# Fewer changes of tile shape on TensorE, a reordered start and a reordered tail in a six-layer cross network

## Chip, cores, metric

One core of one Trainium2 chip. The metric is device time in microseconds (us). All runs quoted are in the fast state. Before: 514.48 us, median of 13 runs (513.51 to 515.35).

## The reference

```python
B, F, D, L = 16384, 26, 16, 6          # Din = 416
def reference(x0, ws, bs):             # x0 (16384, 416), ws (6, 416, 416), bs (6, 416), all bf16
    x = x0
    for l in range(6):
        proj = jnp.einsum('bd,de->be', x, ws[l]) + bs[l]
        x = x0 * proj + x
    return x
```

The activations are kept transposed, with the 416 features on the partitions: 416 = 3 x 128 + 32. The three planes of 128 fill the partitions. The last 32 features of four groups of 512 rows are stacked into one tile of 128 partitions, so four small matmuls can run side by side in different parts of the TensorE array (in the profile of before, eight 32*128 ones take 0.54 us: two passes of 0.216 and a change of tile shape of 0.11).

## The kernel before

The rows are worked in 4 blocks of 4096, each block in two halves q of 2048 rows; 4 blocks x 6 layers x 2 halves = 48 *sets*. A set has four *phases* m: three that make 128 output features each, and one (m = 3) that makes the last 32.

```python
if m == 0:
    ...                                     # wait for x of this set
if m < 3:
    k32_first = (m == 1)
    def full_part(first):                   # "F": 12 matmuls 128*128, 4 banks x 3 planes
        for j in range(4):
            if first: bank_wait(slots[j])
            for c in range(3):
                pe.matmul(pb[:, bk, :], w_sb[:, l, c, 128*m:128*(m+1)], src12[:, c, tcols(q, j)], ...)
    def k32_part(first):                    # "K": 4 matmuls 32*128, side by side
        if first:
            for slot in slots: bank_wait(slot)
        for j in range(4):
            pe.matmul(pb[:, bk, :], w3rep[32*j:32*(j+1), l, 128*m:128*(m+1)],
                      src3[32*j:32*(j+1), pcols(q)], ..., tile_position=(32*j, 0))
    ...                                     # K then F if k32_first, else F then K
else:
    ...                                     # "D": 4 matmuls 32*32, side by side
    ...                                     # then "C": 12 matmuls 128*32, four side by side
mm.then_inc(s_pe, 1)
```

ScalarE (ACT) evicts each phase from PSUM and adds the bias; VectorE (DVE) makes x0 * proj, then adds x, in place. The start and the tail, in the issuing programs:

```python
# scalar: weights, then all staging of the last 32 features (64-byte rows), then the bias
dma_weights(act, 0, s_w0)
dma_staging(act, 0, 0)
dma_staging(act, 0, 1)
act.wait_ge(s_peb, 1); act.activation(bias_f, pb[...], Copy)
# sync: transposed planes of x0
for c in range(3): dma_plane(sp, 0, 0, c)
sp.wait_ge(s_w0, 16 * NW0)
for c in range(3): dma_plane(sp, 0, 1, c)
...
# tail: the last set (set 47) is transposed on TensorE and evicted in 16 pieces, in two halves of 8;
# the set before it (46) is transposed by DMA: 3 planes, then 4 small pieces, then a 640 KB store
for h in range(2):
    for c in range(4):
        ...
        tr = pe.transpose(tb[:, 128*c:128*(c+1)], xT[kbL][:, c, cols], ident128)   # per tile
```

## Time and profile before

| | before |
|---|---|
| time, median | 514.48 us |
| span of the profiled run | 512.5 us |
| TensorE (PE) busy / DVE / ACT | 94% / 73% / 63% |
| first real matmul | 13.96 us |
| steady pair of sets | 2 x 9.94 us |
| tail after the dense stream | 19 us |

"PE" rows are matmuls, and their ends are modelled, so times between matmuls are read from start to start. The profile lines themselves, with how to read them, are shown in the prediction below.

### The profile page before, as it was taken

To read this page: it belongs to the slowest core of one execution; us is meant where nothing else is said; L and a number is where in the kernel's file an instruction comes from. 1 tells how busy PE (TensorE), PEld (TensorE's weight loads), DVE (VectorE), ACT (ScalarE), POOL (GpSimd) and SP (SyncE) were. 2 spreads that over 40 slices of the span, in tenths; PEclk is the share of its full clock that TensorE was granted. 3 is DMA by queue.
4 is the path that set the end of the run, shared out by engine and by line. 5 is a ranking of instruction groups with operands and counts; after the bars stand their busy time and mean duration, and the time that the engine had idled before them with its cause. 6 is when DMAs were issued, how large, how long until landed. Compare 5 with 4: busy or idle time off the path is not lost.

```text
span 512.5 us, 7691 instructions
## 1 busy us (share of the span) xinstructions
PE 480.8 (94%) x3101; PEld 193.6 (38%) x3149; DVE 376.5 (73%) x402; ACT 323.5 (63%) x254; POOL 0.9 (0%) x8
## 2 busy tenths in 40 slices
PE   1999999999999999999999999999999999999972
PEld 0333433433333343343334334333433433343332
DVE  0278779768867877887787788778778877877872
ACT  1366666666667666666766666676666667666651
POOL 0000000000000000000000000000000000000000
PEclk9999999999999999999999999999999999999985
DMA  9869200000975880000669691000459400000186
GB/s 175 189 143 165 62 3 1 0 1 4 207 136 139 177 142 1 1 1 1 123 153 203 117 175 33 0 1 3 82 137 198 119 1 0 2 1 0 20 191 190
DMA packets 149551, 42.26 MB, mean 82 GB/s; under 512 B 130054, under 2 KB 149516, under 8 KB 149516
## 3 DMA queue, kind: packets, MB, share of 16 engines
q1 hardware_dynamic: 144688, 41.07, 39.0%
q10 hardware_dynamic: 4828, 0.69, 0.9%
q8 instruction: 25, 0.41, 0.3%
q14 instruction: 10, 0.08, 0.1%
HBM read 3.61 MB, written 13.63 MB: 34 GB/s over the span
## 4 chain that ended last, share of the span: by engine, by line
PE 93%; issue 2%; DMA 1%; SPq 1%; DVE 1%; DVEq 0%
PE pb L384 74%; PE pb L402 8%; PE pb L434 7%; PE pb L423 3%; DMA x0Ta<-in_x_dram 1%; SPq L171 1%; PE pb L461 1%; DVE xTb L554 0%; DVE x0Ta L580 0%; DVE t1M L540 0%; PE pb L467 0%; DVE t L545 0%; DVEq L184 0%; DVEq L538 0%
## 5 line engine op out<-in xcount | busy, mean ns | idle before, releaser
L497 ACT ACTIVATE projMa<-pb,bias_f 128x2048 bf16<-128x2048 f32 (+1 forms) x90 | 144.4, 1625 | 84.8 <-issue 44.0
L497 ACT ACTIVATE projMb<-pb,bias_f 128x1536 bf16<-128x1536 f32 (+2 forms) x108 | 147.1, 1396 | 78.1 <-issue 45.1
L384 PE MATMUL pb<-xTa,w_sb 128*128 128x512 bf16 x700 | 158.0, 379 | 3.1 <-issue 3.0
L384 PE MATMUL pb<-xTb,w_sb 128*128 128x512 bf16 x700 | 157.8, 379 | 3.2 <-issue 3.2
L384 PEld LDWEIGHTS pb<-xTb,w_sb 128*128 128x128 bf16 x720 | 67.2, 98 | 92.5 <-issue 17.0
L384 PEld LDWEIGHTS pb<-xTa,w_sb 128*128 128x128 bf16 x720 | 67.1, 98 | 92.6 <-issue 17.0
L554 DVE TENSOR_TENSOR xTb<-t1M,xTb 128x2048 bf16<-128x2048 bf16 x60 | 73.2, 1220 | 13.9 <-PE pb L434 13.9
L554 DVE TENSOR_TENSOR xTa<-t1M,xTa 128x2048 bf16<-128x2048 bf16 x60 | 73.2, 1220 | 13.8 <-PE pb L434 13.8
L540 DVE TENSOR_TENSOR t1M<-projMa,x0Ta 128x2048 bf16<-128x2048 bf16 x36 | 43.9, 1219 | 23.0 <-ACT projMa L497 23.0
L540 DVE TENSOR_TENSOR t1M<-projMb,x0Tb 128x2048 bf16<-128x2048 bf16 x36 | 44.0, 1221 | 19.2 <-ACT projMb L497 19.2
L540 DVE TENSOR_TENSOR t1M<-projMb,x0Ta 128x2048 bf16<-128x2048 bf16 x36 | 44.0, 1221 | 18.6 <-ACT projMb L497 18.3
L540 DVE TENSOR_TENSOR t1M<-projMa,x0Tb 128x2048 bf16<-128x2048 bf16 x36 | 43.9, 1220 | 17.4 <-ACT projMa L497 17.4
L384 PE MATMUL pb<-x0Ta,w_sb 128*128 128x512 bf16 x140 | 34.0, 397 | 1.5 <-DMA x0Ta<-in_x_dram 1.1
L384 PE MATMUL pb<-x0Tb,w_sb 128*128 128x512 bf16 x140 | 31.6, 379 | 0.6 <-issue 0.6
L384 PEld LDWEIGHTS pb<-x0Ta,w_sb 128*128 128x128 bf16 x144 | 13.9, 101 | 21.5 <-issue 5.7
L384 PEld LDWEIGHTS pb<-x0Tb,w_sb 128*128 128x128 bf16 x144 | 13.4, 98 | 18.5 <-issue 3.4
L402 PE MATMUL pb<-xT3b,w3rep 32*128 32x512 bf16 x240 | 20.1, 381 | 0.0
L402 PE MATMUL pb<-xT3a,w3rep 32*128 32x512 bf16 x240 | 20.1, 381 | 0.0
L554 DVE TENSOR_TENSOR xTa<-t1M,x0Ta 128x2048 bf16<-128x2048 bf16 x12 | 14.7, 1221 | 3.0 <-PE pb L434 3.0
L434 PE MATMUL pb<-xTb,w_sb 128*32 128x512 bf16 x240 | 16.6, 383 | 0.0
L434 PE MATMUL pb<-xTa,w_sb 128*32 128x512 bf16 x240 | 16.6, 383 | 0.0
L554 DVE TENSOR_TENSOR xTb<-t1M,x0Tb 128x2048 bf16<-128x2048 bf16 x12 | 14.6, 1220 | 2.7 <-PE pb L434 2.7
(54 smaller groups left out, 161.2 us busy)
## 6 DMA issues: line engine op xcount, KB each, us to landing
out_dram<-ostage SPq DMA_DIRECT2D x7, 1024.0 KB, 6.7
out_dram<-ostage SPq DMA_DIRECT2D x7, 640.0 KB, 4.3
out_dram<-x0Ta SPq DMA_DIRECT2D x2, 832.0 KB, 6.8
w_sb<-in_ws_dram SPq DMA_DIRECT2D x5, 312.0 KB, 2.8
st<-in_x_dram SPq DMA_DIRECT2D x24, 32.0 KB, 2.5
w3rep<-in_ws_dram SPq DMA_DIRECT2D x20, 26.0 KB, 2.2
w_sb<-in_ws_dram ACTq DMA_DIRECT2D x1, 312.0 KB
st<-in_x_dram ACTq DMA_DIRECT2D x8, 32.0 KB, 5.6
```

Of the source, the lines that this page charges most:

```text
L171: eng.dma_start_transpose(out=x0T[kb][:, c, qcols(q)], in_=x0[r0:r0 + QC, 128 * c:128 * (c + 1)]).then_inc(s_x0[kb][q], 16)
L384: r = pe.matmul(pb[:, bk, :], w_sb[:, l, c, 128 * m:128 * (m + 1)], src12[:, c, tcols(q, j)], start=(first and c == 0), stop=((not first) ...
L402: r = pe.matmul(pb[:, bk, :], w3rep[32 * j:32 * (j + 1), l, 128 * m:128 * (m + 1)], src3[32 * j:32 * (j + 1), pcols(q)], start=first, stop ...
L423: mm = pe.matmul(pb[32 * j:32 * (j + 1), bk, :], w3rep[32 * j:32 * (j + 1), l, 384:416], src3[32 * j:32 * (j + 1), pcols(q)], start=True, ...
L434: mm = pe.matmul(pb[32 * j:32 * (j + 1), bk, :], w_sb[:, l, c, 384:416], src12[:, c, tcols(q, j)], start=False, stop=(c == 2), tile_positi ...
L461: tr = pe.transpose(tb[:, 128 * c:128 * (c + 1)], xT[kbL][:, c, cols], ident128[:, :])
L497: act.activation(dst, src, ACTF.Identity, bias=bias_f[:, l, m:m + 1], scale=1.0).then_inc(s_act, nb)
L540: dve.tensor_tensor(t1M[:, m, :], projM[par][:, m, :], x0T[kb][:, m, qcols(q)], ALU.mult,).then_inc(s_op1, 1)
L554: dve.tensor_tensor(xT[kb][:, m, qcols(q)], t1M[:, m, :], src12[:, m, qcols(q)], ALU.add,).then_inc(s_dve, 1)
```

## The change

Its intent: let parts with the same tile shape meet, so that TensorE changes shape less often; keep transfers that are not yet needed out of the way of the first ones; and shorten the tail by sending the last 160 columns of set 46 through TensorE too ("hybrid") and by evicting set 47 in one batch of eight double tiles.

```diff
+ORDER, START, HYB, BATCH = 1, 1, 1, 1
+STAGE0, ORDER10, OP3, WARM = 1, 1, 1, 0
+LATE, STAGE1, PLANES = 0, 0, 0
...
-                    for m in range(4):
+                    if not ORDER:
+                        order = [(0, False), (1, True), (2, False), (3, True)]
+                    elif ORDER10 and sidx > 0 and sidx % 2 == 0:
+                        order = [(0, True), (1, False), (2, True), (3, False)]
+                    elif sidx % 2 == 0:
+                        order = [(0, False), (1, True), (2, False), (3, False)]
+                    else:
+                        order = [(3, True), (0, False), (1, True), (2, False)]
+                    for m, small_first in order:
...
                 dma_weights(act, 0, s_w0)
-                dma_staging(act, 0, 0)
-                dma_staging(act, 0, 1)
+                if STAGE0 or not (START or STAGE1):
+                    dma_staging(act, 0, 0)
+                if not (START or STAGE1):
+                    dma_staging(act, 0, 1)
                 act.wait_ge(s_peb, 1)
                 ...                                  # the bias
+                if START or STAGE1:
+                    ...
+                    dma_staging(act, 0, 1)
...
-                sp.wait_ge(s_w0, 16 * NW0)
+                if START or PLANES:
+                    sp.wait_ge(s_x0[0][0], 16 * 3)
+                else:
+                    sp.wait_ge(s_w0, 16 * NW0)
...                                                   # tail, TensorE
+                if HYB:
+                    pe.wait_ge(s_dve, baseH + 4)
+                ...                                   # 16 + 16 transposes of set 46 into 4 banks
+                halves = [range(OSUB)] if BATCH else [range(0, 8), range(8, 16)]
+                ...                                   # set 47, plane by plane, two tiles to a bank
+                if BATCH:
+                    tr.then_inc(s_pt, 1)              # one signal after all 64
...                                                   # tail, ScalarE
+                for g in range(NP46):                 # 4 evictions 128x640 into the staging tile
...                                                   # VectorE: fourth product earlier in odd sets (OP3)
```

More of the change, by code (lines that the diff above doesn't have):

```diff
@@ L82, in bass_standalone__cross_network_dcn__recsys_kernel @@
         s_outB = sem("s_outB")
+        s_p46 = sem("s_p46")
+        s_ev46 = sem("s_ev46")
         s_pt = sem("s_pt")
@@ L87, in bass_standalone__cross_network_dcn__recsys_kernel @@
         phases = []
+        phase_of = {}
         nslot = 0
+        sidx = 0
         for k in range(NBLK):
@@ L95, in bass_standalone__cross_network_dcn__recsys_kernel @@
                         nslot += nb
-                        phases.append(dict(k=k, l=l, q=q, m=m, slots=slots))
+                        ph = dict(k=k, l=l, q=q, m=m, slots=slots, small_first=small_first)
+                        phases.append(ph)
+                        phase_of[(sidx, m)] = ph
+                    sidx += 1
         act_val_after_slot = {}
@@ L114, in bass_standalone__cross_network_dcn__recsys_kernel @@
             ph["act_after"] = acc
-        tslots = list(range(nslot, nslot + OSUB))
-        nslot += OSUB
-        ev_engine = ["A" if jj % 8 in (1, 4, 7) else "D" for jj in range(OSUB)]
+        NP46 = 4 if HYB else 0
+        p46slots = list(range(nslot, nslot + NP46))
+        nslot += NP46
+        NTB = OSUB // 2 if BATCH else OSUB
+        tslots = list(range(nslot, nslot + NTB))
+        nslot += NTB
+        ev_engine = ["D", "A", "D", "D", "A", "D", "D", "A"]
+        if not BATCH:
+            ev_engine = ["A" if jj % 8 in (1, 4, 7) else "D" for jj in range(OSUB)]
         ev_index = []
         na = nd = 0
-        for jj in range(OSUB):
-            if ev_engine[jj] == "A":
+        for i in range(NTB):
+            if ev_engine[i] == "A":
                 ev_index.append(na)
@@ L127, in bass_standalone__cross_network_dcn__recsys_kernel, with op_pos @@
                 nd += 1
-        N_EVA, N_EVD = na, nd
+        def op_pos(s):
+            return (0, 1, 3, 2) if OP3 and s % 2 else (0, 1, 2, 3)
         def slot_free_wait(eng, slot):
@@ L135, in slot_free_wait @@
                 eng.wait_ge(s_act, act_val_after_slot[prev])
-            else:
-                jj = prev - tslots[0]
-                if ev_engine[jj] == "A":
-                    eng.wait_ge(s_evA, ev_index[jj] + 1)
+            elif prev in p46slots:
+                eng.wait_ge(s_ev46, p46slots.index(prev) + 1)
+            else:
+                i = prev - tslots[0]
+                if ev_engine[i] == "A":
+                    eng.wait_ge(s_evA, ev_index[i] + 1)
                 else:
-                    eng.wait_ge(s_evD, ev_index[jj] + 1)
+                    eng.wait_ge(s_evD, ev_index[i] + 1)
         def qcols(q):
@@ L154, in bass_standalone__cross_network_dcn__recsys_kernel @@
         sLAST = NSETS - 1
+        sHYB = set_index(NBLK - 1, L - 1, 0) if HYB else -1
         NOUT = NBLK * NQ
@@ L221, in _ @@
                 ).then_inc(s_bias, 1)
+                if START or STAGE1:
+                    if not STAGE0:
+                        dma_staging(act, 0, 0)
+                    dma_staging(act, 0, 1)
                 act.wait_ge(s_bias, 1)
@@ L249, in _ @@
                             for h in range(2):
-                                na_h = sum(1 for jj in range(8 * h + 8) if ev_engine[jj] == "A")
-                                nd_h = sum(1 for jj in range(8 * h + 8) if ev_engine[jj] == "D")
+                                nh = (h + 1) * (NTB // 2)
+                                na_h = sum(1 for i in range(nh) if ev_engine[i] == "A")
+                                nd_h = sum(1 for i in range(nh) if ev_engine[i] == "D")
                                 sp.wait_ge(s_evA, na_h)
                                 sp.wait_ge(s_evD, nd_h)
+                                if LATE and h == 0:
+                                    sp.wait_ge(s_ev46, 4)
+                                    sp.dma_start(
+                                        out[r0 - QC:r0, 256:D].rearrange("(j a) d -> a j d", a=128),
+                                        ostage[:, :, 256:D],
+                                    ).then_inc(s_outB, 16)
                                 sp.dma_start(
@@ L261, in _ @@
                             continue
-                        last = False
+                        hyb = sL == sHYB
                         base = 4 * sL
@@ L278, in _ @@
                         ntr += 2
-                        if not last:
+                        if not hyb:
                             sp.wait_ge(s_dve, base + 3)
@@ L292, in _ @@
                         n_stA += 1
-                        if not last:
+                        if hyb and LATE:
+                            pass
+                        elif hyb:
+                            sp.wait_ge(s_ev46, 4)
+                            sp.dma_start(
+                                orows[:, 256:D].rearrange("(j a) d -> a j d", a=128),
+                                ostage[:, :, 256:D],
+                            ).then_inc(s_outB, 16)
+                        else:
                             sp.wait_ge(s_dve, base + 4)
@@ L355, in _ @@
                     s = set_index(k, l, q)
-                    if m == 0:
+                    if ip % 4 == 0:
                         if l == 0:
                             pe.wait_ge(s_x0[kb][q], 16 * 3 * (k // 2 + 1))
+                            if m != 0 or ph["small_first"]:
+                                pe.wait_ge(s_c3, NQ * k + q + 1)
                         else:
@@ L374, in _ @@
                     if m < 3:
-                        k32_first = (m == 1)
+                        k32_first = ph["small_first"]
                         def full_part(first):
@@ L394, in k32_part @@
                             r = None
-                            if l == 0 and m == 0:
+                            if l == 0 and ip % 4 == 0 and not first:
                                 pe.wait_ge(s_c3, NQ * k + q + 1)
@@ L421, in _ @@
                         bk = slots[0] % NBANK
-                        for j in range(4):
-                            mm = pe.matmul(
-                                pb[32 * j:32 * (j + 1), bk, :],
-                                w3rep[32 * j:32 * (j + 1), l, 384:416],
-                                src3[32 * j:32 * (j + 1), pcols(q)],
-                                start=True,
-                                stop=False,
-                                tile_position=(32 * j, 32 * j),
-                                skip_group_check=True,
-                            )
@@ L432, in _, with diag_part @@
-                        for c in range(3):
+                        diag_first = ph["small_first"]
+                        def diag_part(first):
+                            r = None
                             for j in range(4):
-                                mm = pe.matmul(
+                                r = pe.matmul(
                                     pb[32 * j:32 * (j + 1), bk, :],
-                                    w_sb[:, l, c, 384:416],
-                                    src12[:, c, tcols(q, j)],
-                                    start=False,
-                                    stop=(c == 2),
-                                    tile_position=(0, 32 * j),
+                                    w3rep[32 * j:32 * (j + 1), l, 384:416],
+                                    src3[32 * j:32 * (j + 1), pcols(q)],
+                                    start=first,
+                                    stop=(not first),
+                                    tile_position=(32 * j, 32 * j),
@@ L441, in _, with col_part @@
                                     skip_group_check=True,
                                 )
+                            return r
+                        def col_part(first):
+                            r = None
+                            for c in range(3):
+                                for j in range(4):
+                                    r = pe.matmul(
+                                        pb[32 * j:32 * (j + 1), bk, :],
+                                        w_sb[:, l, c, 384:416],
+                                        src12[:, c, tcols(q, j)],
+                                        start=(first and c == 0),
+                                        stop=((not first) and c == 2),
+                                        tile_position=(0, 32 * j),
+                                        skip_group_check=True,
+                                    )
+                            return r
@@ L443, in _ @@
+                        if diag_first:
+                            diag_part(True)
+                            mm = col_part(False)
+                        else:
+                            col_part(True)
+                            mm = diag_part(False)
                         mm.then_inc(s_pe, 1)
@@ L447, in _ @@
                 kbL = kL % 2
-                baseL = 4 * sLAST
-                for h in range(2):
-                    for c in range(4):
-                        if h == 0:
-                            pe.wait_ge(s_dve, baseL + c + 1)
-                        for jj in range(8 * h, 8 * h + 8):
-                            slot = tslots[jj]
-                            bk = slot % NBANK
-                            tb = pb[:, bk, :].bitcast(BF16)
-                            if c == 0:
-                                slot_free_wait(pe, slot)
-                            cols = slice(qL * QC + jj * 128, qL * QC + (jj + 1) * 128)
-                            if c < 3:
+                baseH = 4 * sHYB
@@ new lines, in _ @@
+                if HYB:
+                    pe.wait_ge(s_dve, baseH + 4)
+                for g in range(NP46):
+                    slot_free_wait(pe, p46slots[g])
+                for c in (2, 3):
+                    for g in range(NP46):
+                        bk = p46slots[g] % NBANK
+                        tb = pb[:, bk, :].bitcast(BF16)
+                        tr = None
+                        for u in range(4):
+                            jj = 4 * g + u
+                            off = u * 256
+                            if c == 2:
+                                cols = slice(jj * 128, (jj + 1) * 128)
@@ L461, in _ @@
                                 tr = pe.transpose(
-                                    tb[:, 128 * c:128 * (c + 1)], xT[kbL][:, c, cols], ident128[:, :]
+                                    tb[:, off:off + 128], xT[kbL][:, 2, cols], ident128[:, :]
                                 )
                             else:
-                                j = jj // 4
-                                pc = slice(qL * TN + (jj % 4) * 128, qL * TN + (jj % 4 + 1) * 128)
+                                pc = slice((jj % 4) * 128, (jj % 4 + 1) * 128)
@@ L467, in _ @@
                                 tr = pe.matmul(
-                                    tb[:, 384:D],
-                                    xT3[kbL][32 * j:32 * (j + 1), pc],
-                                    ident128[32 * j:32 * (j + 1), 32 * j:32 * (j + 1)],
+                                    tb[:, off + 128:off + 160],
+                                    xT3[kbL][32 * g:32 * (g + 1), pc],
+                                    ident128[32 * g:32 * (g + 1), 32 * g:32 * (g + 1)],
                                     is_transpose=True,
-                                    tile_position=(32 * j, 0),
+                                    tile_position=(32 * g, 0),
@@ L473, in _, with warm @@
                                 )
+                        if c == 3:
+                            tr.then_inc(s_p46, 1)
+                baseL = 4 * sLAST
+                tr = None
+                def warm(n):
+                    for i in range(n):
+                        pe.matmul(
+                            pb[:, tslots[0] % NBANK, 256:512],
+                            w_sb[:, 0, 0, 0:128],
+                            w_sb[:, 0, i % 3, 0:256],
+                            start=True,
+                            stop=True,
+                        )
@@ new lines, in _ @@
+                halves = [range(OSUB)] if BATCH else [range(0, 8), range(8, 16)]
+                for c, jj in [(c, jj) for hv in halves for c in range(4) for jj in hv]:
+                    if jj == 0:
+                        if WARM and c == 0:
+                            slot_free_wait(pe, tslots[0])
+                        if WARM and c < 3:
+                            warm(10 if c == 0 else 8)
+                        pe.wait_ge(s_dve, baseL + c + 1)
+                    if True:
+                        slot = tslots[jj // 2] if BATCH else tslots[jj]
+                        bk = slot % NBANK
+                        off = (jj % 2) * TN if BATCH else 0
+                        tb = pb[:, bk, :].bitcast(BF16)
+                        if c == 0 and (jj % 2 == 0 or not BATCH):
+                            slot_free_wait(pe, slot)
+                        cols = slice(qL * QC + jj * 128, qL * QC + (jj + 1) * 128)
+                        if c < 3:
+                            tr = pe.transpose(
+                                tb[:, off + 128 * c:off + 128 * (c + 1)],
+                                xT[kbL][:, c, cols],
+                                ident128[:, :],
+                            )
+                        else:
+                            j = jj // 4
+                            pc = slice(qL * TN + (jj % 4) * 128, qL * TN + (jj % 4 + 1) * 128)
+                            tr = pe.matmul(
+                                tb[:, off + 384:off + D],
+                                xT3[kbL][32 * j:32 * (j + 1), pc],
+                                ident128[32 * j:32 * (j + 1), 32 * j:32 * (j + 1)],
+                                is_transpose=True,
+                                tile_position=(32 * j, 0),
+                            )
+                            if not BATCH:
@@ L483, in _ @@
                     if s >= 2:
-                        act.wait_ge(s_op1, 4 * (s - 2) + m + 1)
+                        act.wait_ge(s_op1, 4 * (s - 2) + op_pos(s - 2)[m] + 1)
                     col0 = 0
@@ L500, in _ @@
                         col0 += nb
-                for jj in range(OSUB):
-                    if ev_engine[jj] != "A":
+                if HYB:
+                    act.wait_ge(s_outB, 16 * (NOUT - 2))
+                for g in range(NP46):
+                    bk = p46slots[g] % NBANK
+                    tb = pb[:, bk, :].bitcast(BF16)
+                    act.wait_ge(s_p46, g + 1)
+                    act.activation(
+                        ostage[:, 4 * g:4 * (g + 1), 256:D],
+                        tb[:, 0:1024].rearrange("p (u e) -> p u e", e=256)[:, :, 0:160],
+                        ACTF.Copy,
+                    ).then_inc(s_ev46, 1)
+                if BATCH:
+                    act.wait_ge(s_pt, 1)
+                for i in range(NTB):
+                    if ev_engine[i] != "A":
                         continue
-                    bk = tslots[jj] % NBANK
+                    bk = tslots[i] % NBANK
                     tb = pb[:, bk, :].bitcast(BF16)
-                    act.wait_ge(s_pt, jj + 1)
-                    act.activation(ostageL[:, jj, :], tb[:, 0:D], ACTF.Copy).then_inc(s_evA, 1)
+                    if not BATCH:
+                        act.wait_ge(s_pt, i + 1)
+                        act.activation(ostageL[:, i, :], tb[:, 0:D], ACTF.Copy).then_inc(s_evA, 1)
+                        continue
+                    act.activation(
+                        ostageL[:, 2 * i:2 * i + 2, :],
+                        tb[:, 0:1024].rearrange("p (u e) -> p u e", e=TN)[:, :, 0:D],
+                        ACTF.Copy,
+                    ).then_inc(s_evA, 1)
             @block.vector
@@ L533, in _ @@
                     src3 = x0T3[kb] if l == 0 else xT3[kb]
+                    pos = op_pos(s)
                     def op1(m):
-                        dve.wait_ge(s_act, phases[4 * s + m]["act_after"])
+                        dve.wait_ge(s_act, phase_of[(s, m)]["act_after"])
                         if s >= 1:
@@ L551, in op2 @@
                             dve.wait_ge(s_pe, 4 * s + 4)
-                        dve.wait_ge(s_op1, 4 * s + m + 1)
+                        dve.wait_ge(s_op1, 4 * s + pos[m] + 1)
                         if m < 3:
@@ L565, in _ @@
                     op2(0)
+                    if OP3 and s % 2:
+                        op1(3)
                     op1(2)
                     op2(1)
-                    op1(3)
+                    if not (OP3 and s % 2):
+                        op1(3)
                     op2(2)
@@ L573, in _ @@
                         c3_transpose(k + 1, 1)
-                for jj in range(OSUB):
-                    if ev_engine[jj] != "D":
+                if BATCH:
+                    dve.wait_ge(s_pt, 1)
+                for i in range(NTB):
+                    if ev_engine[i] != "D":
                         continue
-                    bk = tslots[jj] % NBANK
+                    bk = tslots[i] % NBANK
                     tb = pb[:, bk, :].bitcast(BF16)
-                    dve.wait_ge(s_pt, jj + 1)
-                    dve.tensor_copy(ostageL[:, jj, :], tb[:, 0:D]).then_inc(s_evD, 1)
+                    if not BATCH:
+                        dve.wait_ge(s_pt, i + 1)
+                        dve.tensor_copy(ostageL[:, i, :], tb[:, 0:D]).then_inc(s_evD, 1)
+                        continue
+                    dve.tensor_copy(
+                        ostageL[:, 2 * i:2 * i + 2, :],
+                        tb[:, 0:1024].rearrange("p (u e) -> p u e", e=TN)[:, :, 0:D],
+                    ).then_inc(s_evD, 1)
 _INS = ['x0', 'ws', 'bs']
```

## The prediction

The sum in it came to 8.1 us, so 506.4. What no trace or run of this case shows is cut, and each cut is marked. One term of the sum: the 0.6, the estimate for a rise of the clock that might come earlier at the start. Without it the terms make 7.5, so 507.0. Rival (b) is that a change of shape between some pairs costs less, or more, than between the rest.

> **What bounds the kernel now.** I began with the page's busy table and its slices.
>
> ```profile
> PE 480.8 (94%) x3101; PEld 193.6 (38%) x3149; DVE 376.5 (73%) x402; ACT 323.5 (63%) x254; POOL 0.9 (0%) x8
> PE   1999999999999999999999999999999999999972
> PE 93%; issue 2%; DMA 1%; SPq 1%; DVE 1%; DVEq 0%
> ```
>
> TensorE (PE) is full from the second slice to the last two, and the third line, the chain that ended last, is TensorE for 93%. The view of waits has no TensorE wait for ScalarE, VectorE or a PSUM bank in the steady part, so only fewer TensorE microseconds, an earlier first matmul or a shorter tail can help. DVE (73%) and ACT (63%) are followers.
>
> Next the timeline of TensorE alone, one steady set (2048 rows of one layer; there are 48):
>
> ```profile
> 203.79 0.40 PE L423 MATMUL pb<-xT3b,w3rep 32*32 32x512 bf16 x4
> 204.12 0.83 PE L434 MATMUL pb<-xTb,w_sb 128*32 128x512 bf16 x12
> 205.11 2.54 PE L384 MATMUL pb<-xTb,w_sb 128*128 128x512 bf16 x11 [0.16 <-issue]
> 207.58 0.61 PE L402 MATMUL pb<-xT3b,w3rep 32*128 32x512 bf16 x8
> 208.12 5.35 PE L384 MATMUL pb<-xTb,w_sb 128*128 128x512 bf16 x24
> 213.41 0.40 PE L402 MATMUL pb<-xT3b,w3rep 32*128 32x512 bf16 x4
> 213.73 0.40 PE L423 MATMUL pb<-xT3b,w3rep 32*32 32x512 bf16 x4
> 214.06 0.83 PE L434 MATMUL pb<-xTb,w_sb 128*32 128x512 bf16 x12
> ```
>
> Read start to start, since matmuls overlap. Call the tile shapes F (128*128), K (32*128), D (32*32) and C (128*32); four K, D or C run side by side and cost one pass. F x24 takes 213.41 - 208.12 = 5.29 us = 24 passes + one change of shape; K x8 takes 208.12 - 207.58 = 0.54 = 2 passes + one change. The difference, 22 passes, is 4.75: a pass is 0.216 us and a change 0.11. A set is 36 F + 3 K + 1 D + 3 C = 43 passes = 9.28, and has 6 changes (F-K, K-F, F-K, K-D, D-C, C-F) = 0.66; the sum, 9.94, is the period seen from 204.12 to 214.06. So a set holds 0.66 us in which nothing is multiplied. That is the only slack inside TensorE.
>
> The start, from the chain in order of time and the DMA view between 12.3 and 13.0 us (packets of a queue, MB, share of 16 engines; packets overlap, so shares pass 100%):
>
> ```profile
> 6.53 7.38 DMA x0Ta<-in_x_dram
> 13.96 4.85 PE pb L384 x12
> q10 hardware_dynamic: 1533, 0.10, 149.8%
> q1 hardware_dynamic: 40, 0.00, 3.9%
> ```
>
> The first matmul waits for the third transposed plane of x0, which lands at 13.9. The next two lines show why so late: the plane's data are moved by about 12.3, but then queue 10, which carries the 64-byte rows of staging, has the engines, and queue 1, with the completion writes of that plane, gets 3.9%. Staging of the second half (q=1), which is not needed yet, stands in front. The second line also shows a half-speed start: 12 passes in 4.85 us where 2.6 are due.
>
> The tail, from the timeline (SPq is the queue that issues transfers) and the windows (us, busy time of PE, PEld, DVE, ACT, POOL, TensorE clock, DMA share, GB/s):
>
> ```profile
> 494.70 6.95 SPq L296 DMA_TRANSPOSE ostage<-xT3b  x4
> 502.80 0.38 SPq L302 DMA_DIRECT2D out_dram<-ostage  x1
> 503.27 2.57 SPq L254 DMA_DIRECT2D out_dram<-x0Ta  x2
> 503.30 1.50 DVE L580 COPY x0Ta<-pb 128x416 bf16<-128x416 bf16 x5 [2.33 <-PE pb L467]
> 496.00:498.00 2.00, 1.03 (x8) 0.77 (x8) 2.00 (x3) 0.00 (x0) 0.00 (x0) 0.52 1.09 314
> 508.00:509.00 1.00, 0.00 (x0) 0.00 (x0) 0.00 (x0) 0.00 (x0) 0.00 (x0) 0.50 1.12 333
> ```
>
> The dense stream ends at T = 493.2 and the span at 512.5, so the tail is 19.3 us. The first half of the last set is evicted by 501.0, but its store leaves only at 503.27: the issuing queue was held by four DMA transposes of the set before and by that set's 640 KB store. From 504 to 511.8 the DMA engines then move 2.3 MB without a hole. TensorE's clock drops to half at about 496[...].
>
> [...]
>
> **The change, part by part.** (1) Order of phases. With | between phases, an even set becomes K F|F K|K F|C D (the very first F K|K F|F K|C D) and an odd one D C|F K|K F|F K. Neighbouring sets now meet D to D and K to K. Changes per pair: K-F, F-K, K-F, F-C, C-D in the even set, D-C, C-F, F-K, K-F, F-K in the odd one: 10 in place of 12. Passes stay 86. In the whole run 48 x 5 = 240 changes replace 48 x 5 + 47 = 287: 47 x 0.11 = 5.2 us, all on the path. I take F-C as costly as C-F (0.11), though the trace has not got it.
>
> Can the followers keep up? I laid one pair out by hand. It takes 86 x 0.216 + 10 x 0.11 = 19.65 us. A phase of a K first needs all four banks at once, freed by the eviction of two phases back (1.97 us, or 2.12 in two pieces). The tightest case: the even set's first phase ends at 2.9, ScalarE is done at about 5.1, and the third phase's K asks at 5.8. The margin is about 0.7 us, and the same elsewhere. On VectorE an even set's last add is done about 15.3 and an odd one's about 6 us into the next pair, each some 4 us before use; the swap of the fourth product in odd sets follows the order in which ScalarE delivers. So nothing is given back here.
>
> (2) Start. Staging of q=1 is issued after the bias, and the q=1 planes only after the q=0 planes have landed. The third plane's completion is then written at about 12.3 and not 13.0: 0.7 us gained. The q=1 planes took from 13.0 to 20.0 and will take until about 22; they are needed at 25, so this is hidden. [...]
>
> (3) Tail, counted from the new T. The last set now ends with an F K phase, whose eviction ends at T+2.1, so VectorE's planes come at T+1.6, 4.5, 5.6 and 6.0 (now T+1.25, 3.5, 5.0, 5.3): later by 0.4 to 1.0. TensorE does 32 transposes of the previous set's last columns in about 1.6 us while it would idle. ScalarE evicts them in 4 x about 0.6 (0.41 per 128x416 now, scaled to 640) by T+4.6. Their 640 KB leave at T+5 rather than T+9.6, with four or five DMA transposes fewer. The last set's 64 transposes come plane by plane: plane 0 done at T+4.8, as half of its banks wait for those ScalarE evictions; planes 1 and 2, 16 x 0.107 each at the half clock, T+6.5 and T+8.2; the small ones T+8.75. All evictions now start there, twice as large: three on VectorE at no more than 2 x 0.284 give the first half at T+10.5. The store's data begin 1.2 us after its issue (502.8 to 504.0 now), 1.7 MB at 325 GB/s take 5.2, and 0.7 passes between the data's end and the span's end: T+17.7 against T+19.3. Gain 1.6.
>
> Sum: 5.2 + 0.7 + 0.6 + 1.6 = 8.1, so 514.5 - 8.1 = 506.4.
>
> **The rivals.** (a) A wait takes the place of the switches: PSUM banks or ScalarE, with a margin of only 0.7 us, stop the K-first phases. Against it: ACT idles a third of the time, and waits for TensorE, not the reverse. If it came, 0.3 us in each pair would cost 7 and the time would be 513. (b) [...] C-F measures 0.11 to 0.12, so I expect no surprise. If F-C were free, 24 x 0.11 = 2.6 more would come: 504. (c) The tail gives back: one semaphore for all 64 transposes puts every eviction after the last of them, where halves overlapped before. If ScalarE's four evictions or the cold clock hold plane 0 longer, the tail's gain is lost: 508. If the clock stays high, planes 1 and 2 take 16 x 0.056 and the tail gains 3.3: 504.7. (d) The later q=1 planes arrive after 25 and open a hole at the second set: 1 to 3 us, 508.
>
> **Range and chances.** The switch term is counted, not guessed, so it carries little spread. [...] the runs of before already spread from 513.5 to 515.0. Eight in ten: 503.4 to 509.2. Faster by 2% means below about 504.3, which needs the clock's help at start or tail: 0.2. Slower is next to excluded, 0.01.
>
> **What would show it.** Right: a steady pair of 19.65 us in TensorE's timeline (39.3 for four sets), D x8 and K x8 at the seams, still no TensorE wait for ACT; first matmul at about 13.2; last store issued at about T+12 and the tail near 17.7. Wrong: holes before L402's successor put down to ACT, a pair still at 19.9, a hole before the second set, or a last eviction later than T+11.6.

## The result

504.3 us, median of 8 runs (502.76 to 505.83). The ratio is 0.9799, with a 95% interval of 0.9785 to 0.9813. Ratios here are the mean time of one kernel's fast runs over that of the other's of the same rounds, so not quite the ratio of the medians quoted. The change is faster by 2.0%, just at the 2% line. The prediction said 506.4, with a range of 503.4 to 509.2.

The page after, busy time and the chain that ended last:

```profile
PE 474.5 (94%) x3133; PEld 190.0 (38%) x3181; DVE 377.3 (75%) x397; ACT 322.8 (64%) x237; POOL 0.9 (0%) x8
PE 89%; ACT 4%; issue 3%; DMA 1%; SPq 1%; DVE 0%; DVEq 0%; ACTq 0%
```

TensorE is still the bound. ScalarE now appears in the chain with 4%, and the first question is whether a wait for it has taken the place of the changes of shape. TensorE's timeline, one steady pair of sets:

```profile
204.51 5.35 PE L442 MATMUL pb<-xTb,w_sb 128*128 128x512 bf16 x24
209.80 0.61 PE L460 MATMUL pb<-xT3b,w3rep 32*128 32x512 bf16 x8
...
216.17 2.76 PE L442 MATMUL pb<-xTb,w_sb 128*128 128x512 bf16 x12
218.86 0.83 PE L500 MATMUL pb<-xTb,w_sb 128*32 128x512 bf16 x12
219.62 0.61 PE L485 MATMUL pb<-xT3b,w3rep 32*32 32x512 bf16 x8
220.16 0.83 PE L500 MATMUL pb<-xTb,w_sb 128*32 128x512 bf16 x12
221.15 2.54 PE L442 MATMUL pb<-xTb,w_sb 128*128 128x512 bf16 x11 [0.16 <-ACT projMa L624]
...
224.17 5.35 PE L442 MATMUL pb<-xTb,w_sb 128*128 128x512 bf16 x24
```

From 204.51 to 224.17 is 19.66 us for a pair; the prediction said 19.65, and before it was 19.88. At the seam inside the pair D meets D (x8 where the kernel before has x4). The 0.16 us "for ACT" in front of x11 is no wait: the row has 11 of 12 matmuls. From the start of C at 220.16 to the start of K, 223.62 in the same view, there is room for 3 + 12 passes of 0.216 and two changes of 0.11, 3.46 us, and no more. Before had the same 0.16 in the same place, put down to "issue". So ScalarE's share of the chain in the steady part is an artefact of one missing record in each pair. (The view of waits counts 23 such gaps, 3.6 us in all; the 4% is larger because the chain goes on from such a gap to the eviction before it.)

The start, from the chain in order of time:

```profile
6.35 5.97 DMA x0Ta<-in_x_dram
12.36 3.86 PE pb L442 x12
```

The first real matmul starts at 12.36, not 13.96, and its twelve passes take 3.86 us, not 4.85. The tail, from the timeline:

```profile
487.34 2.48 ACT L635 ACTIVATE ostage<-pb 128x640 bf16<-128x640 bf16 x4
489.84 0.37 SPq L345 DMA_DIRECT2D out_dram<-ostage  x1
489.87 3.30 PE L583 MATMUL pb<-ident,xTb 128*128 128x128 bf16 x34 [0.20 <-ACT ostage L635]
493.50 2.58 DVE L737 COPY x0Ta<-pb 128x832 bf16<-128x832 bf16 x5 [2.20 <-PE pb L591]
495.16 1.37 SPq L302 DMA_DIRECT2D out_dram<-x0Ta  x2
```

The 640 KB store (L345) now leaves at 489.84, while the last set is still being transposed, and the last stores (L302) find the issuing queue free. Here ScalarE is really in the chain: the last transposes wait for its four evictions.

Where the 10.4 us between the two profiled spans (512.5 and 502.1) came from, with T taken in both as the start of the last group of matmuls plus its passes (493.0 and 485.2; the prediction took 493.2, from the modelled end of the last matmul):

| stretch | before | after | gain |
|---|---|---|---|
| first real matmul | 13.96 | 12.36 | 1.6 |
| from it to the first K | 4.77 | 3.80 | 1.0 |
| from the first K to T | 474.3 | 469.0 | 5.2 |
| tail, T to the end | 19.5 | 16.9 | 2.6 |

(Gains are taken before rounding.)

### The profile page after: what moved, and what is told of

Read it like the earlier page. It is cut to its first block, busy times and chain, and to the rows that moved or that the text cites. A ratio compares the mean times of both kernels' runs of the same rounds, so it can differ in the third digit from the quotient of the medians.

```text
span 502.1 us, 7762 instructions
## 1 busy us (share of the span) xinstructions
PE 474.5 (94%) x3133; PEld 190.0 (38%) x3181; DVE 377.3 (75%) x397; ACT 322.8 (64%) x237; POOL 0.9 (0%) x8
## 4 chain that ended last, share of the span: by engine, by line
PE 89%; ACT 4%; issue 3%; DMA 1%; SPq 1%; DVE 0%; DVEq 0%; ACTq 0%
PE pb L442 75%; PE pb L460 8%; PE pb L500 4%; ACT projMa L624 3%; PE pb L485 1%; DMA x0Ta<-in_x_dram 1%; SPq L202 1%; PE pb L583 1%; ACT ostage L635 0%; DVE x0Ta L737 0%; ACT projMb L624 0%; DVEq L215 0%; PE pb L591 0%; ACTq L611 0%
## 5 line engine op out<-in xcount | busy, mean ns | idle before, releaser
L624 ACT ACTIVATE projMb<-pb,bias_f 128x2048 bf16<-128x2048 f32 (+1 forms) x90 | 144.4, 1625 | 90.4 <-issue 53.6
L689 DVE TENSOR_TENSOR t1M<-projMa,x0Ta 128x2048 bf16<-128x2048 bf16 x36 | 43.7, 1218 | 12.7 <-ACT projMa L624 12.7
L460 PE MATMUL pb<-xT3b,w3rep 32*128 32x512 bf16 x240 | 18.6, 379 | 0.0
L460 PE MATMUL pb<-xT3a,w3rep 32*128 32x512 bf16 x240 | 18.6, 379 | 0.0
L624 ACT ACTIVATE proj3b<-pb,bias_f 128x512 bf16<-128x512 f32 x24 | 16.6, 691 | 0.0
L624 ACT ACTIVATE proj3a<-pb,bias_f 128x512 bf16<-128x512 f32 x24 | 16.4, 682 | 0.0
```

Source lines behind the costliest of these rows:

```text
L460: r = pe.matmul(pb[:, bk, :], w3rep[32 * j:32 * (j + 1), l, 128 * m:128 * (m + 1)], src3[32 * j:32 * (j + 1), pcols(q)], start=first, stop ...
L624: act.activation(dst, src, ACTF.Identity, bias=bias_f[:, l, m:m + 1], scale=1.0).then_inc(s_act, nb)
L689: dve.tensor_tensor(t1M[:, m, :], projM[par][:, m, :], x0T[kb][:, m, qcols(q)], ALU.mult,).then_inc(s_op1, 1)
```

## The experiments

Each kernel is the changed one with one part undone or altered; the change's own switches serve for most. All gave correct results. Ratios are to the kernel before, in the same rounds; a difference of ratios times 514 gives the us between two of them (the intervals are plus or minus 0.14 to 0.28 points, so a difference of two is uncertain by 1.1 to 1.7 us).

### 1. The order of the phases

**order0**: the old order, start and tail new.

```diff
-ORDER, START, HYB, BATCH = 1, 1, 1, 1
-STAGE0, ORDER10, OP3, WARM = 1, 1, 1, 0
+ORDER, START, HYB, BATCH = 0, 1, 1, 1
+STAGE0, ORDER10, OP3, WARM = 1, 0, 0, 0
```

> The changed kernel with the old order of phases (12 changes of tile shape in a pair of sets, and the old order of VectorE's fourth product); start and tail stay new. Theory: each change of shape costs 0.11 us, so the steady pair is 19.88 us, the dense stream 5.2 us longer, the time about 509.5. Rival: part of the gain of the whole change is the better fit of ScalarE and VectorE in the new order, or the changes are cheap and start and tail gave most: then clearly less than 5 us is lost, 505 to 507.

Measured: 508.52 us (6 runs), ratio 0.9903 against 0.9799, so 5.3 us are lost.

**order11**: 11 changes of shape in a pair.

```diff
-STAGE0, ORDER10, OP3, WARM = 1, 1, 1, 0
+STAGE0, ORDER10, OP3, WARM = 1, 0, 1, 0
```

> The changed kernel, but even sets begin with the full matmuls again, so K does not meet K at the seam from an odd to an even set: 11 changes of shape in a pair in place of 10. Theory: steady pair 19.77 us, 23 more changes, 2.5 us longer: about 506.8. Rival (what is saved depends on which shapes meet, a K-K seam saving nothing): 504.3 as the changed kernel.

Measured: 506.84 us (4 runs), ratio 0.9861, 3.2 us above the changed kernel. The steady pair is 19.77 us (TensorE's timeline, 202.93 to 222.70).

**order16**: 16 changes of shape in a pair, the old order with its second phase turned.

```diff
-                        order = [(0, False), (1, True), (2, False), (3, True)]
+                        order = [(0, False), (1, False), (2, False), (3, True)]
```
(and the switches as in order0)

> The old order with the second phase turned round too, so that every phase of full matmuls ends in its small part: 8 changes of shape in a set, 16 in a pair, the same matmuls. Theory: steady pair 86 x 0.216 + 16 x 0.11 = 20.33 us, so 10.6 us more than with the old order, about 520. Rival (the holes come from PSUM or ScalarE, not from changes of shape): not more than the old order, 509 to 511.

Measured: 519.71 us (4 runs), ratio 1.0114: slower than before by 1.1%, and 10.8 us above order0. TensorE's timeline of order16, the C part of two sets, one pair apart:

```profile
206.31 0.83 PE L500 MATMUL pb<-xTb,w_sb 128*32 128x512 bf16 x12
226.62 0.83 PE L500 MATMUL pb<-xTb,w_sb 128*32 128x512 bf16 x12
```

The pair is 20.31 us. The same multiplications, with 10, 11, 12 and 16 changes of shape, take 19.66, 19.77, 19.88 and 20.31 us in a pair: 0.11 us for each change. No pair of shapes that met is cheap: F-C, which the prediction had to assume, can be read in the changed kernel's timeline above, 218.86 - 216.17 = 2.69 us for 12 passes and the change, that is 0.10. The rivals (the fit of ScalarE and VectorE, PSUM waits, a seam that saves nothing) fall. (In the time of the run, order11 lost 3.2 us where 2.5 were due, within the uncertainty.)

### 2. The start

**start0**: the old start, order and tail new.

```diff
-ORDER, START, HYB, BATCH = 1, 1, 1, 1
+ORDER, START, HYB, BATCH = 1, 0, 1, 1
```

> The changed kernel with the old start (all staging issued ahead of the bias, planes of the second half issued when the weights are there); order and tail stay new. My prediction held the start for worth 0.7 us of earlier planes plus 0.6 of expected clock: 505.6. The two profiles say more: first matmul at 13.96 against 12.36, and its first twelve passes 4.85 us against 3.86, together 2.6 us: about 506.9, with the clock rising at 18.4 and not at 14.9.

Measured: 505.91 us (4 runs), ratio 0.9846: the new start is worth 2.4 us, nearly twice what I had predicted. In its profile the first matmul is at 13.64, and the clock record in the packed trace rises at 18.7 (14.6 in the changed kernel's, 18.2 in that of before; the expectation's 18.4 and 14.9 are about 0.2 late).

**stage1** and **planes**: the two parts of the new start, one at a time.

```diff
-ORDER, START, HYB, BATCH = 1, 1, 1, 1
-LATE, STAGE1, PLANES = 0, 0, 0
+ORDER, START, HYB, BATCH = 1, 0, 1, 1
+LATE, STAGE1, PLANES = 0, 1, 0          # planes: 0, 0, 1
```

> The old start with one part of the new: the staging of the second half is issued after the bias; the planes of the second half still wait for the weights only. Theory (the 64-byte rows of that staging are what holds up the third plane): first matmul at about 12.4, time as the changed kernel, 504.3. Rival (the planes of the second half, issued at 10.4, share the engines with the third plane): first matmul stays near 13.9, 506 to 507.

> The old start with the other part of the new: planes of the second half wait until the first three have landed; all staging is issued early, as before. Theory (staging is the cause): nothing gained, first matmul near 13.9, 506.5 to 507. Rival (the planes are the cause): first matmul at about 12.4, 504.3.

Measured: stage1 504.51 us (5 runs), ratio 0.9804; planes 505.93 us (4 runs), ratio 0.9845. So late staging gives the whole gain and late planes give none. TensorE's timeline, stage1 and then planes:

```profile
12.41 4.16 PE L442 MATMUL pb<-x0Ta,w_sb 128*128 128x512 bf16 x12 [0.30 <-DMA x0Ta<-in_x_dram]
```

```profile
13.18 4.88 PE L442 MATMUL pb<-x0Ta,w_sb 128*128 128x512 bf16 x12 [1.05 <-DMA x0Ta<-in_x_dram]
```

What late staging does is finer than I had thought. In the records of single packets the third plane's data are moved by 11.6 in both, and in both the first staging packet of q=1 comes just ahead of their end. But with early staging (planes) the last completion write of the plane comes at 12.06 and the matmul at 13.18; with late staging (stage1) at 11.58 and 12.41. The rate of the staging packets is not what differs at that moment. This is queue 10 in the 0.24 us after the plane's data, in the kernel before (12.09 to 12.33) and in the changed kernel (11.72 to 11.96):

```profile
q10 hardware_dynamic: 550, 0.03, 156.7%
q10 hardware_dynamic: 502, 0.03, 142.7%
```

Only later, 0.2 us and more after the completion was written, do they thin out to a trickle in the changed kernel (DMA view between 11.93 and 12.31 us):

```profile
q10 hardware_dynamic: 372, 0.02, 65.7%
```

In the profiles of before, start0, planes and start0_warm9 all the 32 four-byte packets that end the plane are late, the last by 0.5 to 0.7 us after the data, and the matmul starts 1.1 to 1.3 us after that. In nine profiles with late staging the last follows the data within 0.06 us, and the matmul 0.6 to 0.8 us later. The tenth, halves_prewarm below, shows 0.9 us although its staging was issued late too; there 30 of the 32 are written by 11.83 and the last two at 12.7. So the gain seems to rest on a near miss between two transfers; what holds the writes back is not shown. Why the changed kernel escapes with as many staging packets behind its plane is open.

**start0_warm9**: the old start, planes as late as before, but nine warm-up matmuls in place of six.

```diff
-                NWARM = 6
+                NWARM = 9
```
(and the switches as in start0)

> The old start, with nine warm-up matmuls in place of six, so that TensorE is busy until about 14.0 and the hole of 1.06 us ahead of the first real matmul is closed, while the planes land as late as before. Theory (the clock of the first passes depends on that hole): [...] about 505.5. Rival (the clock rises [...] whatever the hole): no gain against the old start, 507.

Measured: 503.43 us (4 runs), ratio 0.9797: 2.5 us better than start0 and level with the changed kernel, from three dummy matmuls. TensorE's timeline:

```profile
10.40 3.30 PE L399 MATMUL pb<-w_sb 128*128 128x416 bf16 x9
13.64 3.85 PE L442 MATMUL pb<-x0Ta,w_sb 128*128 128x512 bf16 x12
```

The first matmul is as late as in start0 (13.64), but without a hole (an idle stretch of TensorE) ahead of it the twelve passes take 3.85 us, where start0's take 5.25. So 1.4 us between these two profiles come from the clock. One profile does not give the size, though, as the clock rises at a different point in each run. The nine profiles whose first matmul follows the warm-up within 0.12 us range from 3.2 to 4.5 us (halves and batch0 here):

```profile
12.37 3.20 PE L442 MATMUL pb<-x0Ta,w_sb 128*128 128x512 bf16 x12
12.61 4.50 PE L442 MATMUL pb<-x0Ta,w_sb 128*128 128x512 bf16 x12
```

The three with a hole of 1.05 us or more (before, planes, start0) took 4.85 to 5.25, about 1.1 us more on average. The clock records separate them too: the clock rises 0.9 to 3.5 us after the first matmul without such a hole, 4.2 to 5.1 us after it with one. The rest of the 2.5 us, 1.1 us, lies in the tail (15.8 us against start0's 16.9), where this run's clock stayed up:

```profile
491.14 2.22 PE L583 MATMUL pb<-ident,xTb 128*128 128x128 bf16 x34 [0.31 <-ACT ostage L635]
```

The same 34 transposes take 3.30 us in the changed kernel. All runs of start0_warm9 have a mean granted clock of 0.994 or more and all of start0 one of 0.993 or less, so the three matmuls seem to have kept the clock up in the tail too; that is not shown, and why is open.

### 3. The tail

**tail0**: old tail.

```diff
-ORDER, START, HYB, BATCH = 1, 1, 1, 1
+ORDER, START, HYB, BATCH = 1, 1, 0, 0
```

> The changed kernel without its tail: the last columns of the set before the last go out by DMA transposes again, and the last set is evicted in sixteen pieces and two halves. Order and start stay new. Theory: the tail is 19.3 us or, as the last set now ends in a phase whose eviction is late, up to 20.3, against 16.9: 2.4 to 3.4 us lost, 506.7 to 507.7. Rival (the tail gained only because the clock of TensorE happened to be high): about 504.5 to 505.5.

**hyb0**: only the hybrid part undone.

```diff
-ORDER, START, HYB, BATCH = 1, 1, 1, 1
+ORDER, START, HYB, BATCH = 1, 1, 0, 1
```

> The changed kernel, but the last columns of the set before the last go out by DMA transposes again; the last set is still evicted in one batch of eight. Theory (what the tail gained is the issuing queue, no longer held by four DMA transposes and the 640 KB store behind them): the stores of the last set cannot leave before about T+10 and queue behind 640 KB, so the tail is 19 us again and the time 506.5, as with the whole tail undone. Rival (the batch of eight is what gained): 504.3 to 505.

**batch0**: only the batch undone.

```diff
-ORDER, START, HYB, BATCH = 1, 1, 1, 1
+ORDER, START, HYB, BATCH = 1, 1, 1, 0
```

> The changed kernel, but the last set is evicted as before, sixteen pieces in two halves; the hybrid transposes stay. Theory: the first half's store leaves earlier (about T+8.6 against T+10.0), the second later (T+12.4), and the data end where they did: 504.3, within 0.7. Rival (the batch gained): 505.5 or more.

Measured: tail0 506.82 us (4 runs), ratio 0.9862; hyb0 506.61 (4 runs), 0.9857; batch0 503.87 (4 runs), 0.9800. The new tail is worth about 3 us (2.3 between the profiled tails: 19.2 us in tail0 and in hyb0, 16.9 in the changed kernel, 16.8 in batch0). All of it is the hybrid part; the batch of eight gains nothing. The timeline of hyb0:

```profile
485.71 7.02 SPq L352 DMA_TRANSPOSE ostage<-xT3b  x4
...
493.89 0.38 SPq L358 DMA_DIRECT2D out_dram<-ostage  x1
494.70 2.23 SPq L302 DMA_DIRECT2D out_dram<-x0Ta  x2
```

The last stores leave at T+10.3, hardly later than the changed kernel's T+10.0, but they queue behind 640 KB that were issued only 0.8 us before. So the hybrid part pays by moving 640 KB out of the last stretch, rather than by letting the last stores be issued sooner.

**halves**: a version meant to beat both. Two halves of four double tiles, each with its own signal.

```diff
-                halves = [range(OSUB)] if BATCH else [range(0, 8), range(8, 16)]
+                halves = [range(0, 8), range(8, 16)]
...
-                            if not BATCH:
+                            if not BATCH or jj % 8 == 7:
                                 tr.then_inc(s_pt, 1)
-                if BATCH:
-                    tr.then_inc(s_pt, 1)
...                                                  # ScalarE and VectorE, before each eviction
-                if BATCH:
-                    act.wait_ge(s_pt, 1)
+                    act.wait_ge(s_pt, 1 + i // 4)      # VectorE: the same with dve
```

> A version meant to beat both: the changed kernel with the last set's eight double tiles transposed and signalled in two halves of four, so that the first half needs no bank of the previous set's columns and is evicted while the second is transposed. Theory: the first store leaves at about T+8.1 and not T+10.0, the second is there in time, and 1.5 to 2 us are saved: about 502.5. Rival (the second half's transposes and evictions come so late that the DMA engines run dry between the two stores): 503.5 to 504.3.

Measured: 502.12 us (5 runs, 502.04 to 503.48), ratio 0.9778 (0.9758 to 0.9799): the best of all, about 1 us below the changed kernel, though the intervals overlap. Its profile shows the mechanism:

```profile
491.26 1.59 DVE L734 COPY x0Ta<-pb 128x832 bf16<-128x832 bf16 x3 [0.61 <-PE pb L591]
492.92 3.26 SPq L302 DMA_DIRECT2D out_dram<-x0Ta  x2
```

T is 484.5 there, so the first half is evicted from T+6.7 and its store leaves at T+8.4 (the changed kernel: T+8.3 and T+10.0). The tail is 15.7 us against 16.9. The clock has a share in that difference. Where it stayed up, in start0_warm9, the batch of eight had a tail of 15.8 too; where it fell before the last 56 of the 64 transposes, in halves_prewarm below, two halves had 15.8 still, while the batch, with 39 to 52 transposes after the fall, had 16.9 to 17.3 (five profiles). So two halves gain 1.1 us or more where the clock falls early; no profile shows them with the clock up throughout.

**halves_prewarm**: the same, and 100 matmuls of the identity ahead of the weights.

```diff
+                pe.wait_ge(s_ms, 4)
+                for i in range(100):
+                    pe.matmul(pb[:, 6, 0:128], ident128[:, :], ident128[:, :], start=True, stop=True)
                 pe.wait_ge(s_w0, 16 * NW0)
```

> The version with two halves, and 100 transposed-size matmuls of the identity with itself ahead of the wait for the weights, so that TensorE is busy from about 2 us on and its clock is up before the first real matmul. Theory (the first twelve passes run cold because TensorE idled for the first 10 us): they take 2.65 us where the changed kernel's took 3.86, and the time is 1.2 us or more below the version with two halves: about 501. Rival (the clock is bound to something else, or the landing planes set the pace): no gain.

Measured: 504.89 us (5 runs, 502.71 to 506.48), ratio 0.9814: worse than halves by 1.9 us, though the runs overlap. The number that I expected failed, and so did the step from an early clock to fast first passes. TensorE's timeline:

```profile
1.96 8.21 PE L377 MATMUL pb<-ident 128*128 128x128 bf16 x100 [1.96 <-POOL ident L231]
...
10.38 1.23 PE L402 MATMUL pb<-w_sb 128*128 128x416 bf16 x6
13.86 4.45 PE L445 MATMUL pb<-x0Ta,w_sb 128*128 128x512 bf16 x12 [2.26 <-DMA x0Ta<-in_x_dram]
```

The clock did rise early, and in this profile just that undid it: the six warm-up matmuls took 1.23 us instead of 2.26, ended at 11.6, and left a hole of 2.26 us up to a plane that was late too (its last completion write came 0.9 us after the data, as told above). The windows view has the clock at 1.00 until 14, at 0.50 from 14 to 16 and at 0.65 from 16 to 18. So this profile agrees with the clock theory from the wrong side: an early rise was lost again after a hole of 2.26 us ahead of the first real matmul. A pre-warmed kernel with enough warm-up matmuls to reach the landing plane was not run.

## Why the prediction was right, point by point

- **Bound**: right. TensorE stays full, and no follower stops it.
- **Order, 5.2 us**: right in mechanism and size. 47 changes at 0.11 us: 5.2 between the profiles, 5.3 by undoing it. The hand-laid pair (19.65; with the rounded figures as printed the sum is 19.68) measured 19.66. The pass of 0.216 us also held: F x24 takes 5.29 us in the changed kernel too (209.80 - 204.51). Rival (b), a change that costs less between some shapes, is refuted by the line of 10, 11, 12 and 16 changes and by F-C at 0.10; rival (a), PSUM or ScalarE, by a pair without holes.
- **Start, 0.7 + 0.6**: the cause right (early staging), its working only in part, both sizes too small; 2.4 us by undoing it. That queue 10 then has the engines is not what delays the completion: in the changed kernel it has them as much (142.7%) just after the plane. The first term, "The third plane's completion is then written at about 12.3 and not 13.0", measured 11.72 against 12.79, because the data themselves were through 0.4 us earlier. It also missed that the time from the completion write to the matmul shrinks, from 1.2 us to 0.6: 1.6 in place of 0.7. The second, the estimate of a chance that the clock rises earlier, hung on the hole in the profiles at hand and proved too low: after the first matmul the clock rose later in all three profiles with a hole of 1.05 us or more than in the ten with 0.3 us or none. But the 1.0 us that the two profiles show is one draw: without a hole the twelve passes took 3.2 to 4.5 us, with one 4.85 to 5.25. Moreover the planes part, which I counted as part of the reason, gave nothing.
- **Tail, 1.6**: mechanism half right, the size too small; 2.6 between the profiles, 3.2 by undoing it. The first store left at T+10.0 (I had T+10.5), the last at T+11.0 (T+12), and its data were through sooner: from 496.1 to 501.2 in the packet records. From there to the end of the span it is 1.0 us, before and after, and not 0.7. I had named two causes, the issuing queue and the earlier 640 KB; hyb0 shows the second. The batch, which I suspected of giving time back (rival c), is neutral (batch0).
- **Rival (d)**, late planes of q=1: refuted. The weights of layer 1, which wait for those planes, are issued at 21.43, and TensorE's timeline has no hole at the second set.
- **Clock at the tail**: I had the half clock for planes 1 and 2, and the full clock as a rival. Both happen. In the nine quoted and profiled runs of the changed kernel, three have a mean granted clock of 0.995 and took 502.8 to 503.4 us; six have 0.990 or 0.991 and took 504.0 to 505.8. The profiled run is of the second kind. In the profiles the clock record begins only with the rise at the start (18.2 in before, 14.6 in the changed kernel), so this mean tells of the tail. Over 1 us of the spread goes with this clock, and a single look at a tail says little. order0 splits likewise: 508.0 to 508.9 at 0.996, and 510.1 and 510.5 at 0.991 and 0.992. In the changed kernel's tail the clock came up again while only transposes ran on TensorE (from 487.6 to 493.4): the windows view has it at 0.50 from 490 to 492 and at 0.98 from 494 to 496, and in the single records the transposes start 107 ns apart until 492.4 and 56 ns apart from 492.5 on.

```profile
490.00:492.00 2.00, 2.00 (x21) 2.00 (x20) 1.30 (x2) 0.00 (x0) 0.00 (x0) 0.50 0.63 161
494.00:496.00 2.00, 0.00 (x0) 0.00 (x0) 2.00 (x5) 1.88 (x3) 0.00 (x0) 0.98 0.00 0
```

The sum, 8.1, measured 10.3: the two terms at the ends, start and tail, were each a little over half of what came.

## What to carry to other kernels

On a full TensorE, count changes of tile shape as work (0.10 to 0.11 us each here): order the parts so that equal shapes meet, and multiply the changes saved by what two groups of different length show in the trace. At the ends of a kernel, look for a transfer that is not needed yet in front of a completion that is (here the writes then came 0.5 to 0.7 us after the data), and close holes ahead of the first real matmul: here one of 1.05 us or more cost its length and, through the clock, about 1.1 us again. When an issuing queue is held in a tail, ask how many bytes still stand in line behind it; splitting the last evictions into two halves, so that the first store leaves sooner, gained about 1 us here where the clock fell in the tail, and sixteen smaller pieces in place of eight gained nothing.
